# A gated scan that feeds a top-1 mixture of experts: results turned by VectorE in place of TensorE, operands loaded in another order, the routing end reordered

## The chip, the cores and the metric

The kernel runs on one core of a Trainium2 chip. TensorE (PE in the profile) multiplies, VectorE (DVE), ScalarE (ACT) and GpSimd (POOL) do elementwise work, and SyncE (SP) does little but issue transfers. The metric is device time in microseconds of one execution; times before and after are medians of several runs.

## The reference

Two stages follow each other. The first is a decaying linear-attention scan over 4 batches, 8 heads and 768 positions (head width 32, state width 16), in chunks:

```
la  = log(clip(a)); cum = cumsum(la)                 # per chunk
M   = (C @ B.T) * exp(cum_i - cum_j) * causal
y   = M @ x + (C @ state) * exp(cum)
state = exp(sum(la)) * state + sum_j B_j x_j * exp(cum_end - cum_j)
```

Its output, read as 3072 tokens of 256 numbers, goes into eight experts. Each token goes to the expert with the largest logit, in order of arrival, and is dropped beyond the capacity of 768:

```
logits = y @ w_gate;  e = argmax(logits);  gate = softmax(logits)[e]
h   = relu(rows_of_e @ w1[e])          # 256 -> 1024
out[token] = gate * (h @ w2[e])        # 1024 -> 256, put back at the token's row
```

## The kernel before

**Scan.** The work goes over 24 tiles of 128 positions (six per batch), software-pipelined in one loop over `k`: scores and mask of tile k, the product with x of tile k-1, logits and routing of tile k-2. The order of the calls in that loop is the order on every engine (`manual_schedule`). The operands of batch b+1 (`c_n`, `b_n`, `b_s`, the zero-padded `xz`, rows of decays into the tile `both`, rows of `cn` into `cbd`) are issued on SP's queue by `load_part(b + 1, t)` in step t of batch b. Most are `paced`: the transfer waits for the decay product (`ldp`, L392) of the running step. A batch's `b_n` is first read by `scores` (L442), its `xz` by `carry` (L402). The weights of expert 0 are loaded in the same queue in eight pieces, at the steps in `LOADS`; POOL and ACT split the first of them from step 14 on.

**Routing end.** After the last tile, DVE finds each token's expert and slot. A token's slot is turned into two one-hot factors (`hot_a`, `hot_e`, and from the latter `hot_b`), and PE sums their products (`spots`, L836) into the table `who`: for each expert and slot, the token that sits there. The gathers of rows (`fetch`, L169, on POOL's queue) read `who` as indices and `rows_d` in HBM, where each group of tiles has written its rows (L578). The first 128 rows of expert 0 (the "lead") were gathered earlier; `lead_gemm` (L637) and the products at L1111 compute them in single precision in one pass while the rest of the routing runs. Eight matmuls with no use for their result (L1116) follow.

**Experts.** Eight units follow: 296 rows for expert 0, then 424 rows (3 blocks of 128 and one of 40) for each of experts 1 to 7. Operands are split into a high and a low part (`wh`/`wl`, `xh`/`xl`, `hh`/`hl`; ACT makes the high, DVE the low part), and a product is three matmuls: high-high, high-low, low-high. `gemm1` makes eight blocks f of the hidden layer, six matmuls each (L991), through three PSUM banks: ACT writes `hh`, DVE `hl`, and then the bank is free. `gemm2` makes two output halves d, 24 matmuls each (L1015), copied by ACT to `yt` (L1021). Since `yt` has tokens along the free dimension, `finish` turns it back: for each block of 128 tokens two PE transposes (L1061) into PSUM, a DVE multiplication by the gate (L1048) and a scatter of the rows by POOL (L1049). These jobs are the list `after`; `gemm1` of the next unit pops one after each f from 1 on. During `gemm2`, `turned` prepares the next unit's rows (`turned_blocks` is a 32x32 block transpose by DVE of a tile `g4` that came through HBM; then `xh`, `xl`, and with `find` the send targets `oi`), the next weights are split by the list `jobs`, and the rows of the unit after that are gathered. The last unit computes `gemm2` by token (L1073) and has no turn.

## Time and profile before

| | us |
|---|---|
| median of 3 runs (lowest, highest) | 271.59 (270.85, 272.19) |
| the profiled execution, its own time | 269.67 |
| its span in the profile | 267.9 |
| PE busy | 246.7 (92%) |
| DVE busy | 178.6 (67%) |
| ACT busy | 127.6 (48%) |
| POOL busy | 126.5 (47%) |

Times in the profile are microseconds from the span's start. In its rows a line number is a line of the kernel before, followed by the operation, output<-inputs, partitions x elements. A bracket gives the idle time of the engine just before, and what ended it; "issue" stands for a wait for nothing that the profile shows. The scan takes up to about 85 us, the routing end up to about 106 us, the experts the rest.

### The profile page before, as it was taken

What the parts mean: (1) busy time and instruction counts of PE and PEld (TensorE: products, weight loads), DVE (VectorE), ACT (ScalarE), POOL (GpSimd) and SP (SyncE); (2) the same over time, 40 slices, a digit from 0 to 9 for tenths busy, and PEclk for the clock granted to TensorE, in tenths of its full rate; (3) what the DMA queues carried; (4) which work ended last, traced back from release to release, by engine and by line L of the source; (5) the groups of instructions that cost most, each with busy time, mean ns of one, the idle gap of its engine ahead of it and who ended that gap; (6) DMA issues with size and microseconds to landing.
All of it is one profiled execution on the core that took longest, in us unless ns stands there. A gap on an engine that the chain in (4) does not pass through costs nothing.

```text
span 267.9 us, 7098 instructions
## 1 busy us (share of the span) xinstructions
PE 246.7 (92%) x2746; PEld 206.3 (77%) x2747; DVE 178.6 (67%) x453; ACT 127.6 (48%) x289; POOL 126.5 (47%) x165
## 2 busy tenths in 40 slices
PE   7899998799899779999999999999999999999960
PEld 2345655455556777999999999999999999999960
DVE  6699597567795854686695686496496676676210
ACT  2377557358663442573374463383373553644000
POOL 6966225154683154445353485365465385015230
PEclk9999999999999959999999999999999999999995
DMA  6573645956837222494865914853944925101010
GB/s 197 157 193 90 161 112 136 282 157 172 231 129 214 89 97 65 136 348 169 223 260 150 353 52 140 252 231 111 320 158 126 354 75 168 37 2 64 21 46 3
DMA packets 30101, 42.06 MB, mean 157 GB/s; under 512 B 16089, under 2 KB 22075, under 8 KB 28528
## 3 DMA queue, kind: packets, MB, share of 16 engines
q1 hardware_dynamic: 26656, 33.69, 41.1%
q0 software_dynamic: 3280, 7.86, 9.3%
q8 instruction: 23, 0.38, 0.5%
q14 instruction: 14, 0.11, 0.1%
q10 hardware_dynamic: 128, 0.01, 0.0%
HBM read 32.19 MB, written 9.39 MB: 155 GB/s over the span
## 4 chain that ended last, share of the span: by engine, by line
PE 80%; DVE 7%; DMA 3%; issue 3%; ACT 2%; POOL 1%; SPq 0%; POOLq 0%; ACTq 0%; DVEq 0%
PE ps L991 27%; PE ps L1015 23%; PE sp L442 4%; PE ps2f L1073 4%; PE yp L463 4%; PE yp L474 3%; PE pj L481 2%; PE psy L1061 2%; PE dsp L402 2%; PE ps L1111 2%; DMA b_n<-bn 2%; PE ldp L392 1%; DMA c_n<-cn 1%; DVE mz L448 1%; PE yp L412 1%
## 5 line engine op out<-in xcount | busy, mean ns | idle before, releaser
L169 POOL DMA_INDIRECT g<-rows_d,who x28 | 42.7, 1527 | 37.3 <-PE ps L1015 32.6
L994 DVE SCALAR_TENSOR_TENSOR hl<-ps,hh 128x424 fp32r<-128x424 f32 (+1 forms) x64 | 37.3, 583 | 31.5 <-ACT hh L993 31.3
L993 ACT ACTIVATE hh<-ps 128x424 fp32r<-128x424 f32 (+1 forms) x64 | 32.7, 511 | 45.7 <-PE ps L991 45.7
L1049 POOL DMA_INDIRECT out<-yo,oi x31 | 30.6, 987 | 34.1 <-DVE yo L1048 34.1
L1015 PE MATMUL ps<-hh,wh 128*128 128x424 f32 (+1 forms) x112 | 39.0, 348 | 0.0
L1015 PE MATMUL ps<-hh,wl 128*128 128x424 f32 (+1 forms) x112 | 38.8, 346 | 0.0
L1015 PE MATMUL ps<-hl,wh 128*128 128x424 f32 (+1 forms) x112 | 38.7, 346 | 0.0
L991 PE MATMUL ps<-xh,wh 128*128 128x424 f32 (+1 forms) x128 | 36.9, 368 | 0.1
L128 DVE TENSOR_TENSOR wl<-r,wh 128x1024 fp32r<-128x1024 f32 (+1 forms) x32 | 34.9, 1144 | 0.7 <-ACT wh L127 0.7
L991 PE MATMUL ps<-xh,wl 128*128 128x424 f32 (+1 forms) x128 | 34.2, 348 | 0.0
L127 ACT ACTIVATE wh<-r 128x1024 fp32r<-128x1024 f32 (+2 forms) x48 | 34.2, 767 | 0.0
L991 PE MATMUL ps<-xl,wh 128*128 128x424 f32 (+1 forms) x128 | 34.1, 348 | 0.0
L991 PEld LDWEIGHTS ps<-xl,wh 128*128 128x128 f32 x128 | 23.6, 188 | 0.7
L991 PEld LDWEIGHTS ps<-xh,wl 128*128 128x128 f32 x128 | 23.6, 188 | 0.6
L991 PEld LDWEIGHTS ps<-xh,wh 128*128 128x128 f32 x128 | 21.6, 189 | 0.8 <-ACT xh L949 0.4
L1015 PEld LDWEIGHTS ps<-hl,wh 128*128 128x128 f32 x112 | 21.1, 188 | 0.5
L1015 PEld LDWEIGHTS ps<-hh,wh 128*128 128x128 f32 x112 | 21.1, 188 | 0.4
L1015 PEld LDWEIGHTS ps<-hh,wl 128*128 128x128 f32 x112 | 21.0, 188 | 0.4
L448 DVE TENSOR_TENSOR mz<-sp,lx 128x512 f32<-128x512 f32 x24 | 16.5, 686 | 5.3 <-PE sp L442 3.7
L367 POOL TENSOR_TENSOR bpt<-b_s,wt 128x128 f32<-128x128 f32 x22 | 10.0, 455 | 20.9 <-PE dsp L402 20.9
L476 ACT ACTIVATE ys<-yp 128x128 f32<-128x128 f32 x48 | 10.7, 275 | 18.2 <-PE yp L474 18.2
L442 PE MATMUL sp<-cbd,b_n 64*64 64x256 f32 x176 | 15.5, 401 | 2.0 <-issue 1.6
(190 smaller groups left out, 437.9 us busy)
## 6 DMA issues: line engine op xcount, KB each, us to landing
r<-w SPq DMA_DIRECT2D x12, 1024.0 KB, 6.5
r<-w SPq DMA_DIRECT2D x16, 256.0 KB, 5.3
g<-xr_d SPq DMA_DIRECT2D x24, 112.0 KB
rows_d<-rt SPq DMA_DIRECT2D x5, 514.0 KB
xr_d<-g SPq DMA_DIRECT2D x6, 385.5 KB
xz<-x SPq DMA_DIRECT2D x6, 256.0 KB, 6.4
c_n<-cn SPq DMA_DIRECT2D x3, 384.0 KB, 3.2
b_s<-bt SPq DMA_DIRECT2D x3, 384.0 KB, 5.1
```

The source lines that it names most:

```text
L127: act.activation(hi[:, sl], r[:, sl], AF.Copy)
L128: engine.tensor_tensor(out=lo[:, sl], in0=r[:, sl], in1=hi[:, sl].bitcast(F32), op=ALU.subtract)
L169: got = pool.indirect_dma_start(out=g[0:r, s], out_offset=None, in_=rows_d[0:known, :], in_offset=bass.IndirectOffsetOnAxis(ap=index[0:r, ...
L442: pe.matmul(sp[64 * c:64 * c + 64, g, 0:4 * CH], nat(b, "bn", ts.start, ts.stop)[gp], cbd[b % 2][gp, :, ts], start=True, stop=True)
L448: dve.tensor_tensor(out=m.rearrange("p (g h) i -> p g h i", g=2), in0=sp[:, :, 0:4 * CH].rearrange("p g (h i) -> p g h i", h=4), in1=lx.re ...
L463: step[0] = pe.matmul(yps[g][32 * hh:32 * hh + 32, c * CH:(c + 1) * CH], x_z[:, c, h * D:(h + 1) * D], m[:, h], start=c == 0, stop=False, ...
L991: mm = pe.matmul(ps, wv[:, k, fs], xv[:, k], start=i == 0, stop=i == 5)
L993: act.activation(hh[:, f, 0:w], ps, AF.Relu)
L994: dve.scalar_tensor_tensor(out=hl[:, f, 0:w], in0=ps, scalar=0.0, in1=hh[:, f, 0:w].bitcast(F32), op0=ALU.max, op1=ALU.subtract)
L1015: mm = pe.matmul(ps, wv[:, f, ds], hv[:, f, 0:w], start=f == 0 and j == 0, stop=f == NF - 1 and j == 2)
L1049: sc = pool.indirect_dma_start(out=out, out_offset=bass.IndirectOffsetOnAxis(ap=oi[0:r, s:s + 1], axis=0), in_=yo[0:r], in_offset=None, bo ...
L1073: pe.matmul(ps, hv[:, f, sl], wv[:, f, :], start=f == 0 and j == 0, stop=f == NF - 1 and j == 2)
```

## The change

1. `load_part` issues `bt` and `cn` in step 0, `bn` in step 1, and the second part of `xz` in step 4. `LOADS` puts two pieces of expert 0's weights at steps 6 and 7 and the other six at steps 14 to 19.
2. The routing end is written in another order. The last two groups (three tiles and one) share one `hots_of` over four tiles; `hot` can give its two halves to two engines; the last group's rows are written from ACT's queue; all of `lead_gemm` is ahead of the last `spots`; two idle matmuls are added ahead of the last positions.
3. The send targets of all experts are made at once (`oi_all`) ahead of the first unit, together with a cleared `yt_all`; `find` and its four DVE instructions per unit go.
4. `turn` (PE transposes of the rows of units 0 and 1) fills both halves block by block and stores afterwards.
5. `finish` is no longer used for the units. ACT writes `yt_all` padded to 448 columns, DVE turns each half in 32x32 blocks into `yb`, and `assemble` moves the blocks to their partitions with 16 copies of 32 partitions (eight on ACT, eight on DVE, four per job), then four jobs multiply by the gate (DVE and ACT in turn) and scatter. `gemm1` pops from f = 0.
6. The first job of the weight split runs in `turned`, between the block transpose and `xh`.

```diff
-LOADS = (10, 11, 16, 17, 18, 19, 20, 21)
+LOADS = (6, 7, 14, 15, 16, 17, 18, 19)
...
     def turn(g, w, bank, store):
+        both = [bank(w) for k in range(2)]
+        for s in range(-(-w // P)):
+            r = min(P, w - s * P)
+            for k in range(2):
+                pe.transpose(out=both[k][:, s * P:s * P + r], in_=g[0:r, s, k * P:(k + 1) * P], identity=ident[0:r, 0:r])
         for k in range(2):
...
+            store(k, both[k])
...
-            for nm in ((("cn",), ("bt",)) + ((),) * 4)[t]:
+            for nm in ((("bt", "cn"), ("bn",)) + ((),) * 4)[t]:
                 paced(out=loads[b][nm], in_=src_of[nm][:, b])
-            if t in (1, 3):
-                load_xz(b, t // 2, pace=True)
...
-                paced(out=loads[b]["bn"], in_=bn[:, b])
+            if t in (1, 4):
+                load_xz(b, t // 4, pace=True)
...
-        def hot(n0, T, a_, eq, engine):
+        def hot(n0, T, a_, eq, *engines):
...
-                engine.tensor_tensor(out=b_[:, :, v], in0=eq, in1=bc(parts_of[:, n0:n0 + T, v:v + 1], [P, T, E * ks]), op=ALU.mult)
+                engines[v % len(engines)].tensor_tensor(out=b_[:, :, v], in0=eq, in1=bc(parts_of[:, n0:n0 + T, v:v + 1], [P, T, E * ks]), op=ALU.mult)
...
-        weave(mid, [lambda: None, lambda: None] + late)
+        weave(mid, [lambda: None, lambda: None] + late[:-2])
+        warm = p1.tile([P, CBW], F32, name="warm", tag="yp0")
+        for _ in range(2):
+            pe.matmul(warm, ones, cb_s[:, 0:CBW], start=True, stop=True)
...
-        for op in mid[:3]:
+        for op in (mid[0], mid[2], mid[1], mid[3], mid[5], *late[-2:]):
             op()
         last = route_2(*last, at_of(2, E).rearrange("p (t e) -> p t e", t=1))
-        route_3(*last)
+        act.activation(rt[:, 0, 0:DM], pj[:, 0:DM], AF.Copy)
+        route_3(*last, act)
         late = take()
+        for op in (late[1], late[3], late[5]):
+            op()
         while hots:
             list_(*hots.pop(0))
-        lead_gemm()
-        weave(mid[3:], late)
-        hots.append(hot(*known[0], pool))
-        hots.append(hot(*known[1], dve))
+        while lead_f:
+            lead_gemm()
+        both = hots_of(k - 3, 4)
+        for op in (mid[4], late[4], mid[6], late[6], *both[0:3], late[0], late[2], *both[3:]):
+            op()
+        hots.append(hot(*known[0], dve, pool))
...
-        while lead_f:
-            lead_gemm()
...
                     turned_blocks(xt, g4)
+                    if early:
+                        early.pop(0)()
                     act.activation(xh, xt[:, :, 0:w], AF.Copy)
...
-                    if f >= (4 if rush else 1) and after:
+                    if f >= (4 if rush else 0) and after:
                         after.pop(0)()
...
-                    act.activation(yt[:, d], ps, AF.Copy)
-                return yt
+                    act.activation(yt[:, d, 0:w], ps, AF.Copy)
+                    dve.transpose(out=yb[:, d, 0:n], in_=yt[:, d])
+                return yb
...
+            def assemble(yb, w, gate, oi):
+                nf, blocks = -(-w // Q), -(-w // P)
+                y4 = gp.tile([P, blocks, DM], F32, name="y4", bufs=1)
+                src = yb.rearrange("p k (s r c) -> p k s r c", r=4, c=Q)
+                dst = y4.rearrange("p s (k q c) -> p k s q c", k=2, q=4)
+                todo = []
+                for i in range(16):
+                    q, r = divmod(i, 4)
+                    n = -(-(nf - r) // 4)
+
+                    def move(to=dst[r * Q:(r + 1) * Q, :, 0:n, q], of=src[q * Q:(q + 1) * Q, :, 0:n, r], i=i):
+                        if i % 2:
+                            dve.tensor_copy(to, of)
+                        else:
+                            act.activation(to, of, AF.Copy)
+                    todo.append(move)
+                moves = [lambda some=todo[i:i + 4]: [m() for m in some] for i in range(0, 16, 4)]
+                return moves + [lambda s=s, r=min(P, w - s * P): put(y4[:, s], gate, oi, s, r, True) for s in range(blocks)]
...
+                yt_all = gp.tile([P, 2, quarters * Q], F32, name="yt_all", bufs=1)
+                dve.memset(yt_all, 0.0)
+                oi_all = gp.tile([P, E, KW], I32, name="oi_all", bufs=1)
+                dve.tensor_copy(oi_all, who.rearrange("p (e s) -> p e s", e=E)[:, :, 0:KW])
+                if lead:
+                    dve.tensor_copy(oi_all[:, 0, 0:KW - 1], who[:, 1:KW])
+                for i in range(E):
+                    dve.copy_predicated(oi_all[:, i], dead[:, i], nowhere)
...
-                    cur = turned(g_n, *nxt, four.pop(u + 1, None))
                     if nxt[0] != e:
                         jobs = split_weights(nxt[0], *raws[nxt[0]][1:], wpools[nxt[0] % 2])
+                    cur = turned(g_n, *nxt, four.pop(u + 1, None), jobs)
...
-                    after = finish(yt, w, gate, oi)
+                    after = assemble(yb, w, gate, oi)
```

The order of the instructions shows three places. First SP's queue in the scan, where batch 2 is loaded (steps 6 to 11); before:

```order
L338 DMA c_n<-cn 128x768
L338 DMA b_s<-bt 128x768
L338 DMA xz_103<-x 64x512 x2
L220 DMA both<-cums 1x48x64 x6
L353 DMA cbd_101<-cn 16x768 x4
L338 DMA b_n<-bn 128x768
L578 DMA rows_d<-rt 128x4x257
L338 DMA xz_103<-x 64x1024 x2
L338 DMA r<-w 128x512 x2
```

and now:

```order
L339 DMA b_s<-bt 128x768
L339 DMA c_n<-cn 128x768
L339 DMA r<-w 128x512
L339 DMA b_n<-bn 128x768
L339 DMA xz_103<-x 64x512 x2
L339 DMA r<-w 128x512
L221 DMA both<-cums 1x48x64 x6
L352 DMA cbd_101<-cn 16x768 x4
L588 DMA rows_d<-rt 128x4x257
L339 DMA xz_103<-x 64x1024 x2
```

`b_n` has moved ahead of ten small transfers, and the two weight pieces from behind the second `xz` to places ahead of it.

Second, PE at the routing end, the piece around `lead_gemm` (`lead_p`) and the last `spots`; before:

```order
L637 MATMUL lead_p_2177<-lead_h,r 128x128 x4
L836 LDWEIGHTS hot_a
L836 MATMUL spots<-hot_b,hot_a 128x48
...
L857 MATMUL cnt<-lead_run,cb_s 128x8
L637 MATMUL lead_p_2223<-lead_h,r 128x128 x4
L1111 MATMUL ps_2289<-lead_h,r 128x128 x8
```

and now:

```order
L643 MATMUL lead_p_2179<-lead_h,r 128x128 x4
L643 MATMUL lead_p_2185<-lead_h,r 128x128 x4
L844 LDWEIGHTS hot_a
L844 MATMUL spots<-hot_b,hot_a 128x48
...
L870 MATMUL cnt<-lead_run,cb_s 128x8
L1159 MATMUL ps_2294<-lead_h,r 128x128 x8
```

One group of lead matmuls has moved from behind `cnt` to ahead of the last `spots`.

Third, DVE in `gemm1`, where the results of the unit before are put in place; before (unit 2, counted from 0, takes in the results of unit 1):

```order
L994 SCALAR_TENSOR_TENSOR hl<-ps_2756,hh 128x424
L1048 TENSOR_SCALAR yo<-psy,gate 128x256
L994 SCALAR_TENSOR_TENSOR hl<-ps_2774,hh 128x424
L1048 TENSOR_SCALAR yo<-psy,gate 128x256
L994 SCALAR_TENSOR_TENSOR hl<-ps_2791,hh 128x424
```

and now:

```order
L1038 STREAM_TRANSPOSE yb<-yt_all 128x448
L1008 SCALAR_TENSOR_TENSOR hl<-ps_2750,hh 128x424
L1087 COPY y_2739<-yb 32x2x4x32
L1087 COPY y_2739<-yb 32x2x3x32
L1008 SCALAR_TENSOR_TENSOR hl<-ps_2763,hh 128x424
L1087 COPY y_2739<-yb 32x2x4x32
```

Between two `hl` there were 0 or 1 other instructions; now there are two copies in each of the first four gaps and 0 or 1 after that. ACT has the same two copies behind `hh`.

57 lines of the change are left out of this document (32 added, 25 removed).

## The prediction

> **What bounds the kernel now.** I read the page's engine totals, then a table by stretch, then the chain of waits in order of time for the longest stretch, and the instruction rows for the others.
>
> ```profile
> PE 246.7 (92%) x2746; PEld 206.3 (77%) x2747; DVE 178.6 (67%) x453; ACT 127.6 (48%) x289; POOL 126.5 (47%) x165
> 48.00:62.00 14.00, 12.44 (x297) 7.26 (x291) 9.69 (x34) 7.40 (x25) 4.32 (x10) 1.00 0.72 199
> 94.00:95.00 1.00, 0.20 (x1) 0.10 (x1) 0.96 (x4) 0.00 (x0) 0.86 (x2) 0.62 1.01 346
> 96.00:97.00 1.00, 1.00 (x7) 1.00 (x7) 0.00 (x0) 0.00 (x0) 0.00 (x0) 0.50 0.00 0
> 101.00:102.00 1.00, 1.00 (x11) 1.00 (x10) 1.00 (x2) 0.27 (x1) 0.69 (x2) 0.96 0.15 41
> 150.40:169.80 19.40, 19.40 (x106) 18.61 (x105) 13.57 (x24) 9.78 (x16) 11.61 (x8) 1.00 0.48 164
> ```
>
> In a stretch's row stand its length, then PE, PEld, DVE, ACT and POOL busy, and the granted clock. In the experts (last row) PE is busy 19.40 of 19.40 us: a unit costs what PE's instructions cost. In the scan PE lacks 1.56 us of 14. At the routing end it idles around 94 us, and from there to about 101 us it has half its clock.
>
> ```profile
> 121.10 2.33 PE ps L991 x12
> 123.65 1.16 PE ps L991 x6
> 140.17 2.32 PE ps L991 x12
> 142.71 1.16 PE ps L991 x6
> 144.09 1.16 PE ps L991 x6
> 145.47 1.16 PE ps L991 x6
> 146.85 3.45 PE ps L991 x18
> ```
>
> This is the chain in `gemm1`. The first piece at 140.17 ends at 142.49, the next starts at 142.71: 0.22 us for a pair of PE transposes, four times a unit.
>
> **Turn back (part 5).** The page of groups by shape counts the transposes removed, and prices what DVE and ACT do instead:
>
> ```profile
> L1061 PE MATMUL psy<-hd_s,yt 128*128 128x128 f32 x42 | 8.0, 271 | 0.0
> L1061 PE MATMUL psy<-hd_s,yt 128*40 128x128 f32 x14 | 2.7, 272 | 0.0
> L994 DVE SCALAR_TENSOR_TENSOR hl<-ps,hh 128x424 fp32r<-128x424 f32 x56 | 33.6, 599 | 28.9 <-ACT hh L993 28.7
> L245 DVE TENSOR_SCALAR cbd<-hd_s 128x256 f32<-128x256 f32 x4 | 1.1, 343 | 0.0
> L160 DVE STREAM_TRANSPOSE xt<-g 128x896 f32<-128x896 f32 x6 | 6.7, 1109 | 3.7 <-DMA g<-xr_d 3.7
> L993 ACT ACTIVATE hh<-ps 128x424 fp32r<-128x424 f32 x56 | 29.4, 525 | 41.6 <-PE ps L991 41.6
> L499 ACT ACTIVATE rt<-pj 128x256 f32<-128x256 f32 x23 | 8.9, 386 | 8.7 <-PE pj L481 6.6 <-PE pj L497 1.8
> ```
>
> There are 56 transposes; two belong to the lead and stay. The other 54 are 27 pairs. At 0.22 us they are 5.9 us of PE time, all on the chain.
>
> What replaces them runs beside PE. For DVE a unit gets two transposes of 448 (half of 1109 ns each, 1.1 us in all) and eight copies of up to 256 elements. No copy between partition groups is in the trace; the nearest row is L245, 343 ns, so 2.7 us. It loses two of four gate products (about 1.0) and four `find` instructions (about 0.7). DVE comes from 13.6 to some 15.7 us of 18.5. ACT gains eight copies and two products at about 386 ns: 9.8 + 3.9 = 13.7 us. Neither is full over a unit, but four gaps are. There PE makes a block in 1.16 us, while DVE needs 0.60 + 2 x 0.34 = 1.28 and ACT 0.53 + 2 x 0.39 = 1.31, less what neighbours overlap. DVE falls behind by 0.12 a block, 0.5 us in four. Three PSUM banks allow for more:
>
> ```profile
> 159.57 2.33 PE ps L991 x12
> 161.39 0.60 DVE L994 SCALAR_TENSOR_TENSOR hl<-ps,hh 128x424 fp32r<-128x424 f32 x1 [1.62 <-ACT hh L993]
> ```
>
> The first `hl` ends at 161.99, 2.42 us after the unit began; PE needs that bank for the fourth block, 3 x 1.16 = 3.48 us after it. The slack is about 1.05 us. So I cost the copies at nothing. Bounds of a copy: 0.2 us (no lag), and 0.69 us, the row of 512 elements with two inputs, L448 below, at which DVE lags 0.82 a block, 3.3 us in four, and PE loses 3.3 - 1.05 = 2.2 us a unit, 13 us in six.
>
> ```profile
> L448 DVE TENSOR_TENSOR mz<-sp,lx 128x512 f32<-128x512 f32 x24 | 16.5, 686 | 5.3 <-PE sp L442 3.7 <-PE pj L481 1.4
> ```
>
> I take the 256-element row since the size is the same. The weight split ahead of `xh` (part 6) fills the 0.98 us in which DVE waits for `xh`, and no one waits for it: term 0. Sum of this part: -5.9, from -6.2 to +7.
>
> **Loads (part 1).**
>
> ```profile
> 28.80 0.78 PE L442 MATMUL sp<-cbd,b_n 64*64 64x256 f32 x8 [0.39 <-DMA b_n<-bn]
> 47.45 0.78 PE L442 MATMUL sp<-cbd,b_n 64*64 64x256 f32 x8 [1.15 <-issue]
> 54.12 0.38 PE L402 MATMUL dsp<-xz,bpt 128*32 128x128 f32 x2 [1.36 <-issue]
> 70.38 0.65 PE L442 MATMUL sp<-cbd,b_n 64*64 64x256 f32 x4 [0.45 <-issue]
> 35.52 4.72 SPq L220 DMA_DIRECT2D both<-cums  x6
> 40.29 2.14 SPq L353 DMA_DIRECT2D cbd<-cn  x4
> 42.53 1.04 SPq L338 DMA_DIRECT2D b_n<-bn  x1
> ```
>
> PE waits 0.39 us for the first `b_n`. The 1.15 us at 47.45 have no releaser, but stand at the first instruction of batch 2's `scores`, 3.9 us after `b_n` was issued (43.57). I read that as `b_n` too. It is now issued ahead of 4.72 + 2.14 us of small transfers, so both waits go: 1.5 us. The 1.36 and 0.45 us lie in the middle of a group whose first instructions had run, so they aren't operands; I leave them. The second `xz` has a later step, but SP is behind its steps: its queue came to `xz` at 44.21 and `b_n` ahead of it took 1.04. The weight pieces ahead of the small transfers cost SP 0.4 us each and hide there. Term -1.5; bounds +1 (as much as the wait it cures, where a weight piece or `xz` now ends last) and -3.3 (all four waits).
>
> **Routing end (parts 2 to 4).**
>
> ```profile
> 92.35 1.14 PE L637 MATMUL lead_p<-lead_h,r 128*128 128x128 f32 x8
> 94.58 0.20 PE L836 MATMUL spots<-hot_b,hot_a 128*128 128x48 bf16 x1 [1.09 <-POOL hot_b L597]
> 95.52 2.05 PE L637 MATMUL lead_p<-lead_h,r 128*128 128x128 f32 x8
> 98.12 5.23 PE L1111 MATMUL ps<-lead_h,r 128*128 128x128 f32 x32 [0.55 <-ACT got L860]
> 104.65 1.12 PE L156 MATMUL ps<-hd_s,g_first 128*128 128x128 f32 x6
> 105.25 0.97 ACT L949 ACTIVATE xh<-ps 128x296 fp32r<-128x296 f32 x2 [1.58 <-PE ps L156]
> 105.76 0.96 DVE L950 TENSOR_TENSOR xl<-ps,xh 128x296 fp32r<-128x296 f32 x2 [3.71 <-issue]
> 93.28 0.37 SPq L578 DMA_DIRECT2D rows_d<-rt_last  x1
> 99.95 1.15 POOL L169 DMA_INDIRECT g_first<-rows_d,who  x1 [0.30 <-DVE lead_oi L876]
> DMA to landing us min/median/max: 2.9/3.1/3.3
> ```
>
> The group of 2.05 us moves into PE's idle 1.09 us, so L1111 can start about 1.5 us earlier, at 96.6. From 98.12 to the end of the turn (105.77) are 7.65 us: 104.2. The last gather of `g_first` starts at 99.95 and lands by 103.2 (the last row), and perhaps 0.5 us earlier, since the last rows' reciprocal is five short instructions further ahead. So PE still ends last. If the clock stayed up, the lead's 2.05 would be 1.14 again and L1111 shorter by about as much in proportion (half of three halved microseconds, 1.5); then the gather would end it, near 103.2. The new `turn` has both halves ready at its end, so the second `xh` no longer runs beside it: +0.4. Range of the gain: 0 (`who` late) to 2.2; I take 1.7. The cleared `yt_all` and the targets are some 2.5 us of DVE, in the 3.71 us in which it idles ahead of `xl`; without that cover they would cost up to 2.5.
>
> [...]
>
> **Sum.** -5.9 - 1.5 - 1.7 = -9.1. The profiled execution took 269.67 us, of which 267.9 are the span: 260.6. It was 1.9 us below the median of the runs, 271.59; on the median's scale 262.5.
>
> **Rivals.**
> 1. *DVE's filled gaps set the pace.* For it: 1.28 against 1.16 us, and the copies' price is a guess. Against: 1.05 us of slack, and five lighter gaps after the four. With copies of 0.55 us the lag is 4 x 0.54 = 2.2, the loss 1.1 us a unit, 6.6 in six: 271.6 - 9.1 + 6.6 = 269.1.
> 2. *Only the transposes go.* Loads and gathers end as before, as the unexplained waits and the gather at 99.95 allow: 271.6 - 5.9 = 265.7.
> 3. *Slower: GpSimd and the copies exclude each other.*
>
> ```profile
> 213.99 4.61 DVE L128 TENSOR_TENSOR wl<-r,wh 128x1024 fp32r<-128x1024 f32 x4
> 214.57 4.91 POOL L169 DMA_INDIRECT g<-rows_d,who  x1 [1.26 <-PE ps L1015]
> 219.79 0.95 POOL L169 DMA_INDIRECT g<-rows_d,who  x1 [0.30 <-issue]
> ```
>
> A gather that takes 0.95 us otherwise took 4.91 beside four DVE instructions, and the last gather runs into the next `gemm1`, which begins at 217.7. If a copy there had to wait for such a gather, DVE would lag by up to 4 us; beyond the slack 3 us a unit, 18 in six: 271.6 - 9.1 + 18 = 280. It is slower from a loss of 1.5 us a unit on, a wait of 2.6. Against it: in these rows POOL waited, and DVE's four took their usual time. [...]
>
> **Chances.** Forecast 0.62 (its own range 259.5 to 265), rival 1 0.13, rival 2 0.13, rival 3 0.06, something that leaves the time alone 0.06. The range reaches from 259.0 (loads -3.3, end -2.2, transposes -5.9 less the median's scatter) to 268.0, over rival 2 and half of rival 1. About 0.5% (1.4 us) is what a measurement can tell from no change. Faster: 0.62 + 0.13 + most of rival 1, 0.87; same 0.07; slower 0.06.
>
> **What would show it.** In the profile after: a unit of 18.5 us with no gap between blocks of `gemm1`; copies near 0.34 us, and `hl` less than 1 us later at the fifth block; no wait ahead of `scores` of tiles 6 and 12; L1159 beginning near 96 us less what the scan won; last gather before the turn. The forecast is wrong if PE waits for `hl` in `gemm1` (copies too dear), if waits of the scan come back at other instructions, or if the end of the routing is set by the gather at its old distance.

## The result

The changed kernel takes 261.0 us (median of four runs: 259.1, 260.1, 261.9 and 263.8), the kernel before 271.9 us beside it (270.9 to 274.6). The ratio is 0.956, with a 95% interval from 0.945 to 0.967. The prediction was 262.5 us, within 259.0 to 268.0. Ratios and their intervals, here and below, leave out every execution that took over 1.5% longer than the fastest of its kernel, so they are not the quotients of the medians. The profiled execution is the longest of the four, 263.77 us with a span of 261.9; it has half the TensorE clock for 10 us at the routing end. Against the profiled execution before (span 267.9) it gains 6.0 us.

Line numbers move with the edit: `gemm1` L991 is now L1005, `gemm2` L1015 is L1031, the lead's end L1111 is L1159, `lead_p` L637 is L643, `hl` L994 is L1008, the gather L169 is L170. New are the DVE transpose L1038, the copies L1087 (DVE) and L1089 (ACT), and the products L1068 (DVE) and L1066 (ACT). First the engine totals of the profile after, then two stretches (length, then PE, PEld, DVE, ACT and POOL busy, granted clock): the scan's stretch that stood in the prediction, and one unit of the experts.

```profile
PE 242.7 (93%) x2694; PEld 203.3 (78%) x2695; DVE 189.3 (72%) x484; ACT 153.6 (59%) x358; POOL 125.5 (48%) x164
```

```profile
48.00:62.00 14.00, 13.03 (x349) 7.93 (x348) 10.55 (x40) 8.71 (x29) 5.68 (x14) 1.00 0.66 185
138.00:156.60 18.60, 18.60 (x98) 18.01 (x97) 15.16 (x28) 13.67 (x25) 9.39 (x7) 1.00 0.63 196
```

A unit costs 18.6 us where it cost 19.4, and PE is still busy in all of it. DVE is at 15.2 of 18.6 us and ACT at 13.7 (forecast 15.7 and 13.7). The groups by shape show what the copies cost:

```profile
L1087 DVE COPY y<-yb 32x256 f32<-32x256 f32 x24 | 6.8, 285 | 0.7
L1087 DVE COPY y<-yb 32x192 f32<-32x192 f32 x28 | 7.1, 254 | 0.5
L1089 ACT ACTIVATE y<-yb 32x256 f32<-32x256 f32 x24 | 9.9, 414 | 0.9 <-DVE yb L1038 0.5
L1089 ACT ACTIVATE y<-yb 32x192 f32<-32x192 f32 x28 | 10.1, 360 | 0.3
```

**Where the 6.0 us of the two profiles lie.** The scan ends (first `lead_p` group) at 86.13 instead of 87.64: -1.5. From there to the first `gemm1` it takes 18.45 us instead of 18.08: +0.4. From there to PE's last matmul 147.8 instead of 153.1: -5.3. What follows takes 9.5 instead of 9.1: +0.4, whose cause stays open.

**The scan.** These are the waits of PE without a releaser that are left in the profile after; behind them stands what the transfer queue named "instruction" moved in the window from 82.3 to 83.4 us (packets, MB, share):

```profile
31.61 0.45 PE L474 MATMUL yp<-ct,state 32*64 32x64 f32 x10 [0.76 <-issue]
52.18 0.38 PE L402 MATMUL dsp<-xz,bpt 128*32 128x128 f32 x2 [0.54 <-issue]
84.72 0.31 PE L463 MATMUL yp<-mz,xz 128*32 128x64 f32 x6 [1.42 <-issue]
```

```profile
q8 instruction: 1, 0.02, 5.5%
```

No `scores` waits any more. All three waits stand inside a group whose first matmuls had run. The second is 0.8 us shorter than its like before, the third 0.9 us longer; in sum such waits take 2.7 us here and 2.3 before. The transfer of a piece of 16 KB in that queue (22 of them, 0.36 MB, in the whole profile) ends 1.4 to 1.5 us before each of them does. The author read these pieces as PE's program; the experiments return to this.

**The routing end.** First the clock by stretch in the profile after, then rows of PE and the last gather of `g_first` in order of time:

```profile
81.89:85.31 3.42, 2.00 (x56) 1.72 (x55) 1.32 (x7) 0.84 (x4) 0.00 (x0) 1.00 0.47 173
85.31:95.55 10.24, 9.49 (x66) 8.80 (x57) 6.14 (x39) 2.69 (x13) 0.97 (x2) 0.50 0.30 101
95.55:104.58 9.03, 7.47 (x67) 6.37 (x65) 6.29 (x30) 4.00 (x11) 6.36 (x6) 1.00 0.20 53
```

```profile
86.13 2.08 PE L643 MATMUL lead_p<-lead_h,r 128*128 128x128 f32 x8 [0.46 <-ACT lead_h L632]
97.28 3.84 PE L1159 MATMUL ps<-lead_h,r 128*128 128x128 f32 x32 [0.31 <-ACT got L871]
100.59 1.49 POOL L170 DMA_INDIRECT g_first<-rows_d,who  x1 [0.30 <-issue]
103.83 0.31 PE L156 MATMUL ps<-hd_s,g_first 40*128 40x40 f32 x2 [0.81 <-DMA g_first<-rows_d,who]
```

The wait of 1.42 us leaves PE busy for 2.00 of 3.42 us, and from the end of that stretch on it has half the clock for 10.24 us, at the very place where the closing order was to become denser. Each `lead_p` group takes 2.1 us instead of 1.1, and the last gather, not PE, ends the routing end.

**One unit lost.** In the last unit of this execution the tokens came late. Rows of DVE, of ACT and of PE's weight loads:

```profile
225.50 1.11 DVE L161 STREAM_TRANSPOSE xt<-g 128x896 f32<-128x896 f32 x1 [2.52 <-SPq L1221]
233.22 0.55 DVE L1008 SCALAR_TENSOR_TENSOR hl<-ps,hh 128x424 fp32r<-128x424 f32 x1
234.69 0.60 DVE L1008 SCALAR_TENSOR_TENSOR hl<-ps,hh 128x424 fp32r<-128x424 f32 x1 [0.34 <-ACT hh L1007]
236.06 0.60 DVE L1008 SCALAR_TENSOR_TENSOR hl<-ps,hh 128x424 fp32r<-128x424 f32 x1 [0.18 <-ACT hh L1007]
234.14 0.53 ACT L1007 ACTIVATE hh<-ps 128x424 fp32r<-128x424 f32 x1
234.69 0.79 ACT L1089 ACTIVATE y<-yb 32x256 f32<-32x256 f32 x2
235.50 0.53 ACT L1007 ACTIVATE hh<-ps 128x424 fp32r<-128x424 f32 x1
238.07 0.30 PEld L1005 LDWEIGHTS ps<-xh,wh 128*128 128x128 f32 x2 [0.29 <-DVE hl L1008]
```

`xt` starts 5.4 us before the unit's first matmul (230.90), where in four of the five others it is 7.3 to 8.0. The first `hl` is then late, and since ACT needs 0.53 + 0.79 us and a little idle time for a filled block, `hl` follows at 1.36 to 1.37 us a block beside PE's 1.16. PE waits, and the unit takes 21.2 us, where later kernels show 20.7 for it on time (both up to the start of PE's last group of matmuls). `hl` has the same pace in units on time; there it starts early enough that PE does not wait.

### The profile page after: what moved, and what is told of

Same layout as the page of the kernel before. It is cut to its first block, busy times and chain, and to the rows that moved or that the text cites. A ratio compares the mean times of both kernels' runs of the same rounds, so it can differ in the third digit from the quotient of the medians.

```text
span 261.9 us, 7081 instructions
## 1 busy us (share of the span) xinstructions
PE 242.7 (93%) x2694; PEld 203.3 (78%) x2695; DVE 189.3 (72%) x484; ACT 153.6 (59%) x358; POOL 125.5 (48%) x164
## 5 line engine op out<-in xcount | busy, mean ns | idle before, releaser
L1069 POOL DMA_INDIRECT out<-yo,oi_all x31 | 32.2, 1037 | 56.8 <-DVE yo L1068 50.4
L1008 DVE SCALAR_TENSOR_TENSOR hl<-ps,hh 128x424 fp32r<-128x424 f32 (+1 forms) x64 | 37.2, 582 | 14.7 <-ACT hh L1007 13.8
L170 POOL DMA_INDIRECT g<-rows_d,who x28 | 40.2, 1437 | 13.2 <-PE ps L1031 6.9
L1031 PE MATMUL ps<-hl,wh 128*128 128x424 f32 (+1 forms) x112 | 39.0, 348 | 0.0
L1031 PE MATMUL ps<-hh,wh 128*128 128x424 f32 (+1 forms) x112 | 39.0, 348 | 0.0
L1031 PE MATMUL ps<-hh,wl 128*128 128x424 f32 (+1 forms) x112 | 38.9, 347 | 0.0
L1005 PE MATMUL ps<-xh,wh 128*128 128x424 f32 (+1 forms) x128 | 34.9, 353 | 0.4 <-ACT xh L960 0.4
L127 ACT ACTIVATE wh<-r 128x1024 fp32r<-128x1024 f32 (+2 forms) x48 | 34.8, 767 | 0.1
L1005 PE MATMUL ps<-xl,wh 128*128 128x424 f32 (+1 forms) x128 | 34.5, 350 | 0.0
L1005 PE MATMUL ps<-xh,wl 128*128 128x424 f32 (+1 forms) x128 | 34.3, 349 | 0.0
L1005 PEld LDWEIGHTS ps<-xh,wh 128*128 128x128 f32 x128 | 23.4, 188 | 2.2 <-DVE hl L1008 0.8
L1005 PEld LDWEIGHTS ps<-xl,wh 128*128 128x128 f32 x128 | 23.7, 188 | 0.7
L1005 PEld LDWEIGHTS ps<-xh,wl 128*128 128x128 f32 x128 | 23.7, 188 | 0.5
L1089 ACT ACTIVATE y<-yb 32x192 f32<-32x192 f32 (+2 forms) x56 | 21.3, 380 | 1.3 <-DVE yb L1038 0.5
L1031 PEld LDWEIGHTS ps<-hh,wl 128*128 128x128 f32 x112 | 21.1, 188 | 0.6
L1031 PEld LDWEIGHTS ps<-hh,wh 128*128 128x128 f32 x112 | 21.0, 188 | 0.6
L1031 PEld LDWEIGHTS ps<-hl,wh 128*128 128x128 f32 x112 | 21.1, 188 | 0.4
```

The source lines that it names most:

```text
L127: act.activation(hi[:, sl], r[:, sl], AF.Copy)
L170: got = pool.indirect_dma_start(out=g[0:r, s], out_offset=None, in_=rows_d[0:known, :], in_offset=bass.IndirectOffsetOnAxis(ap=index[0:r, ...
L1005: mm = pe.matmul(ps, wv[:, k, fs], xv[:, k], start=i == 0, stop=i == 5)
L1008: dve.scalar_tensor_tensor(out=hl[:, f, 0:w], in0=ps, scalar=0.0, in1=hh[:, f, 0:w].bitcast(F32), op0=ALU.max, op1=ALU.subtract)
L1031: mm = pe.matmul(ps, wv[:, f, ds], hv[:, f, 0:w], start=f == 0 and j == 0, stop=f == NF - 1 and j == 2)
L1069: sc = pool.indirect_dma_start(out=out, out_offset=bass.IndirectOffsetOnAxis(ap=oi[0:r, s:s + 1], axis=0), in_=yo[0:r], in_offset=None, bo ...
```

## The experiments

Twelve further runs were made, in three sets, each set on one chip; one of them is the changed kernel once more. "Lead to gemm1" is the time from the first `lead_p` group to the first `gemm1`. "Late" is the loss of units against 18.6 us (20.7 for the last), from the starts of `gemm1` in the profiled execution.

| kernel | median us, before beside it | ratio (95%) | first lead_p | lead to gemm1 | late, us |
| --- | --- | --- | --- | --- | --- |
| before (first profile) | 271.6 | | 87.64 | 18.08 | units of 19.4 |
| changed | 261.0, 271.9 | 0.956 (0.945 to 0.967) | 86.13 | 18.45 | 0.5 |
| TensorE turns back | 269.8, 273.6 | 0.984 (0.980 to 0.989) | 86.75 | 18.78 | units of 19.45 |
| old loads | 265.6, 273.6 | 0.963 (0.958 to 0.968) | 86.43 | 19.54 | 1.1 |
| old end | 266.5, 273.6 | 0.974 (0.971 to 0.978) | 86.65 | 18.70 | 2.4 |
| turn back alone | 269.3, 273.6 | 0.983 (0.977 to 0.988) | 92.35 | 18.83 | 0.6 |
| changed again | 265.4, 273.3 | none | 89.10 | 18.47 | 2.4 |
| three a gap | 261.3, 273.3 | 0.965 (0.954 to 0.976) | 87.14 | 15.82 | 0.1 |
| copies on DVE | 271.7, 273.3 | 0.997 (0.990 to 1.004) | 85.67 | 15.85 | units of 20.16 |
| code shift | 262.4, 273.3 | 0.968 (0.954 to 0.983) | 88.03 | 15.85 | 1.1 |
| late split | 266.1, 272.7 | 0.977 (0.968 to 0.986) | 85.16 | 15.84 | 3.6 |
| before, code shift | 270.9, 272.7 | 1.003 (0.996 to 1.011) | 89.01 | 18.70 | units of 19.4 |
| three a gap, shift | 263.9, 272.7 | 0.978 (0.973 to 0.983) | 89.31 | 15.94 | 1.3 |
| loads alone | 271.9, 272.7 | 1.004 (0.993 to 1.014) | 87.52 | 22.12 | units of 19.4 |

### The first set: one part undone, one part alone

TensorE turns back (loads, end and early split as changed):

```
-                    if f >= (4 if rush else 0) and after:
+                    if f >= (4 if rush else 1) and after:
...
-                    dve.transpose(out=yb[:, d, 0:n], in_=yt[:, d])
-                return yb
+                return yt
...
-                    after = assemble(yb, w, gate, oi)
+                    after = finish(yb, w, gate, oi)
```

> The changed kernel with its results turned back by TensorE again (transposes in four gaps of gemm1, no DVE transposes and no copies); loads, routing end, weight split and oi_all as changed. Theory (the turn back is worth the gaps it fills): a unit takes 19.35 us again instead of 18.6, six units 4.5 us, and the time is 0.973 to 0.980 of the kernel before (265.5 us beside 271.9; by the prediction's 5.9 us for 27 pairs 266.9). Rival (the units shrank for another reason, the weight split ahead of xh or the targets made at once): units stay near 18.6 us and the ratio near 0.956. For the last unit, which gained nothing in the changed kernel: if the copies cost it what the transposes had cost, PE no longer waits for hl at its blocks 5 to 7 and it takes 21.7 us all the same; if its xt is late for another reason, the waits stay and it takes about 0.7 us longer.

Ratio 0.984. Units take 19.45 us again and the last one 21.56. On-time units of the changed code take 18.58 to 18.63 and 20.7 us (its first two 14.69 and 18.58, here 14.69 and 19.22); summed over the eight, the transposes cost 5.7 us, 0.21 us a pair. The theory holds for the units, and the rival falls: it is the turn back that shrank the units. The ratio is a little above the expected 0.973 to 0.980.

Old loads (the changed kernel with LOADS and load_part of before):

```
-LOADS = (6, 7, 14, 15, 16, 17, 18, 19)
+LOADS = (10, 11, 16, 17, 18, 19, 20, 21)
...
-            for nm in ((("bt", "cn"), ("bn",)) + ((),) * 4)[t]:
+            for nm in ((("cn",), ("bt",)) + ((),) * 4)[t]:
...
```

> The changed kernel with the loads of before (LOADS and load_part); all else as changed. Theory of the prediction: the two waits ahead of scores of tiles 6 and 12 come back, 0.4 and 1.15 us, and the time is 1.5 us above the changed kernel, 0.961 of the kernel before. Rival (the new stalls in the middle of groups, 0.76 us near 31.6 and 1.42 us near 84.7 in the changed kernel, are the price of the new order of loads): those two go when the loads go back, and the ratio is 0.956 or lower.

Ratio 0.963; its interval overlaps that of the changed kernel, so it does not price the loads. The profiled execution also had half the clock for 3.4 us in its first unit, which took 16.2 us instead of 14.7. One of the two waits came back, twice as long; the other did not. The stalls inside groups stayed (1.09, 1.15 and 0.67 us), so they aren't the price of the new loads. The first row is of this kernel, the next two are of the kernel with the turn back alone, which has the old loads too:

```profile
29.24 0.78 PE L443 MATMUL sp<-cbd,b_n 64*64 64x256 f32 x8 [0.82 <-DMA b_n<-bn]
```

```profile
31.57 0.78 PE L442 MATMUL sp<-cbd,b_n 64*64 64x256 f32 x8 [3.01 <-DMA b_n<-bn]
51.25 0.78 PE L442 MATMUL sp<-cbd,b_n 64*64 64x256 f32 x8 [0.88 <-issue]
```

The wait for `b_n` varies from 0.4 to 3.0 us between executions with the old loads. The two without a releaser at the first `scores` of batch 2 (1.15 us before, 0.88 here) aren't waits for program: the last piece had come 4.2 and 3.8 us before they ended. The wait for `b_n` is in none of the ten profiles with the new loads (in one of these, the changed kernel again, `scores` waits 0.91 us for `cbd`).

Old end (the changed kernel with the closing order, the queue of the last rows and the turn of before):

```
-        weave(mid, [lambda: None, lambda: None] + late[:-2])
-        warm = p1.tile([P, CBW], F32, name="warm", tag="yp0")
-        for _ in range(2):
-            pe.matmul(warm, ones, cb_s[:, 0:CBW], start=True, stop=True)
+        weave(mid, [lambda: None, lambda: None] + late)
...
-        hots.append(hot(*known[0], dve, pool))
+        hots.append(hot(*known[0], pool))
+        hots.append(hot(*known[1], dve))
...
```

> The changed kernel with the routing end of before (order of the closing instructions, queue of the last rows, no two idle matmuls, turn of the first tokens half by half). Theory of the prediction: gemm1 of the first unit begins 1.7 us later and the time is 1.7 us above the changed kernel, 0.962 of the kernel before. Rival 1 (what the new end wins in order it loses to the half clock): no difference, 0.956. Rival 2 (the clock at the end is set by the stall near 84 us, not by the closing order): the clock in the stretch from 82 to 102 us differs from execution to execution in both kernels, and with it the end, by more than 1.7 us.

Ratio 0.974, five us above the changed kernel's by the ratios, more than any theory gave. The profile shows two differences. From the first lead group to `gemm1` it takes 18.70 us, 0.25 more than the changed execution. And its third unit takes 20.96 us: `xt` starts only 3.5 us ahead, and PE waits for `wl`, then for `hl`.

```profile
140.09 0.46 PE L993 MATMUL ps<-xh,wl 128*128 128x424 f32 x1 [0.24 <-DVE wl L128]
143.93 0.66 PE L993 MATMUL ps<-xh,wh 128*128 128x424 f32 x2 [0.67 <-DVE hl L996]
```

So this run doesn't price the closing order by itself, and beside the 0.971 that the changed kernel has in the second set it is hardly slower. Why the tokens of that unit came later with the old end stays open.

Turn back alone (the kernel before with the DVE transposes, the copies and their buffers):

```
-                    yt = gemm2(e, w, hh, hl, jobs)
-                    after = finish(yt, w, gate, oi)
+                    yb = gemm2(e, w, hh, hl, jobs)
+                    after = assemble(yb, w, gate, oi)
...
```

> The kernel before with the turn back alone (DVE transposes, sixteen copies in the first four blocks, product and scatter in the last four); loads, routing end, find per unit and the weight split behind xl as before. Theory: six units of 18.6 us instead of 19.35, 4.4 us (5.9 by the prediction), ratio 0.978 to 0.984. Rival (the copies need the lighter DVE of the other edits: targets made at once save four short instructions a unit, and the earlier split evens its load): PE waits for hl in gemm1, units of 19 us or more, ratio 0.99 or above.

Ratio 0.983. Units take 18.41 to 18.60 us, but for one of 19.05 (its `xt` began 7.1 us ahead), so the copies do not need the other edits. The scan of this execution ended 4.7 us later than that of before (3.0 us went to the `b_n` above, and twice in it the clock was halved for 3.4 us), so that the span was equal to that of before, while from the first `gemm1` on PE ended 5.6 us sooner; without the late unit that is 6.1.

### The second set: slack, pace, code

The changed kernel once more, with no edit:

> The changed kernel once more, beside the three below on one chip, for a second profile. Theory (the time that the scatter of its runs spans comes from the half clock near 85 us and from late tokens of single units): the ratio is again 0.956 within 0.01, units without a wait for hl take 18.5 to 18.6 us, and a unit that takes longer has a DVE transpose of xt that waited over 2 us for a DMA. Rival (the slow last unit belongs to the kernel): unit 7 again has PE waiting for hl in its fifth to eighth block and no late xt.

On this chip it took 265.4 us (260.9 to 268.6), beside 273.3. That is 0.971 by the medians, with no interval, and not the expected 0.956 within 0.01. The eight runs of the changed kernel on two chips have a median of 262.9 us. The theory holds for the units: those on time take 18.6 us, and the three slow ones (19.01, 19.41, and the last with 21.86) have an `xt` that began 5.5, 5.0 and 4.7 us ahead. The scan shows something new, in rows of PE and POOL:

```profile
74.78 0.53 PE L402 MATMUL dsp<-xz,bpt 128*32 128x128 f32 x8 [2.13 <-POOL bpt L367]
73.15 1.13 POOL L170 DMA_INDIRECT lead_h<-rows_d,lead_slot  x1 [3.94 <-DVE sel L595]
74.30 0.42 POOL L367 TENSOR_TENSOR bpt<-b_s,wt 128x128 f32<-128x128 f32 x1
```

The lead's gather starts 2 us after its list is there (`lead_slot`, 70.83), and `bpt` stands behind it on POOL. It reads `rows_d`, whose last part SP issued at 65.56, right ahead of three weight pieces. The landing of these rows took 6.7 us, as the line of their issue says:

```profile
rows_d<-rt SPq DMA_DIRECT2D x1, 514.0 KB, 6.7
```

They landed at 72.3, behind the list, and the gather began 0.9 us later. The same wait is 1.67 us in the code shift and 1.47 with three a gap and the shift, where the rows landed 0.4 and 0.2 us behind the list (7.3 and 7.6 us after their issue) and the gather began 0.9 us after the landing as well; it is 0.28 in the other profiles with the new loads (in that of the changed kernel the rows took 6.6 us and were there 0.9 us ahead of the list). In all three the clock was halved for 3.4 us soon behind that wait. That the weight pieces made the rows late is not shown.

Three copies a block (3, 3, 3, 3, 4 instead of 4, 4, 4, 4):

```
-                moves = [lambda some=todo[i:i + 4]: [m() for m in some] for i in range(0, 16, 4)]
+                cut = (0, 3, 6, 9, 12, 16)
+                moves = [lambda some=todo[i:j]: [m() for m in some] for i, j in zip(cut, cut[1:])]
```

> The sixteen copies in five blocks of gemm1 (three, three, three, three and four) where the changed kernel has four blocks of four; the four products follow one block later. By the rows of the kernels run so far a block with four copies takes ACT 0.53 + 0.79 = 1.32 us and DVE 0.60 + 0.55 = 1.15, beside 1.16 for PE; with three ACT has 1.1 to 1.2. Theory (ACT's filled blocks cannot catch up, so that a unit whose tokens came late stays at 1.36 us a block for all four): late units lose at most 0.3 us instead of 0.5 to 0.8, the others nothing, and the time is that of the changed kernel less 0 to 1 us. Rival (the copies cost nothing in any unit): no difference at all, and the later products and scatters push the gathers of the next tokens back: 0 to 1 us longer.

261.3 us. Tokens that began 5.4 and 5.2 us ahead cost 0 and 0.1 us, where with four copies a block 5.4 and 5.0 us ahead cost 0.5 and 0.8. So a part of what a late unit pays is the filled blocks; not all of it, as tokens 4.05 us ahead cost 1.3 us with three copies a block as well (below). In time it can't be told from the changed kernel.

All copies on DVE:

```
-                        if i % 2:
-                            dve.tensor_copy(to, of)
-                        else:
-                            act.activation(to, of, AF.Copy)
+                        dve.tensor_copy(to, of)
```

> All sixteen copies of a unit on DVE, none on ACT, else the changed kernel. DVE then needs 0.60 + 4 x 0.285 = 1.74 us a block beside 1.16 for PE: a lag of 0.58 a block, 2.3 us in four. Theory of the prediction (three banks give a slack of 1.05 us): PE waits for hl in the fourth to sixth block and a unit takes 1.2 to 1.3 us longer, 19.85 us; six units 7.5 us, ratio 0.98 to 0.985. Rival 1 of the prediction with no slack at all: 2.3 us a unit, 14 us, slower than before. The other end (only DVE's sum over a unit counts, 18.1 of 18.6 us): nothing, 0.956.

```profile
139.41 0.60 DVE L1008 SCALAR_TENSOR_TENSOR hl<-ps,hh 128x424 fp32r<-128x424 f32 x1
140.04 1.11 DVE L1086 COPY y<-yb 32x256 f32<-32x256 f32 x4
141.18 0.60 DVE L1008 SCALAR_TENSOR_TENSOR hl<-ps,hh 128x424 fp32r<-128x424 f32 x1
143.60 0.65 PE L1005 MATMUL ps<-xh,wh 128*128 128x424 f32 x2 [0.34 <-DVE hl L1008]
145.39 0.65 PE L1005 MATMUL ps<-xh,wh 128*128 128x424 f32 x2 [0.36 <-DVE hl L1008]
```

`hl` comes every 1.77 us, PE needs 1.165. At the fifth block `hl` is 2.3 us late (the first step is 1.65 us). Units take 20.16 us, 1.56 more than 18.6 and more than the expected 1.2 to 1.3. The slack is 2.3 - 1.56, about 0.75 us. The slack of three banks is real but smaller than the 1.05 of the prediction, and the ratio of 0.997, above the expected 0.98 to 0.985, is what rival 1 of the prediction looks like when copies are dear: the whole gain is gone.

Part of the difference is a reading in the prediction. It counted the first `hl`'s end (161.99) from 159.57, where a piece of the chain begins, but the unit began at 159.41:

```profile
159.41 0.55 PE L991 MATMUL ps<-xh,wh 128*128 128x424 f32 x2
```

From there the first `hl` ends after 2.58 us, and the same sum gives 3.48 - 2.58 = 0.90.

Code shift (178 more instructions of PE at the start, the rest unchanged):

```
-        keep_warm(WARM, "lj")
+        keep_warm(WARM - 7, "lj")
+        small = p1.tile([P, 512], F32, name="small", tag="lj")
+        for i in range(96):
+            pe.matmul(small[0:32, 0:64], warm_s[:, 0:32], warm_s[:, 0:64], start=True, stop=True)
```

> Seven of the nineteen idle matmuls at the start are replaced by 96 of 64 columns, which take about the same time; nothing else is changed, and PE's program is 178 instructions longer ahead of the scan. Theory (the stalls in the middle of a group, with no releaser, are PE waiting for its program, which comes in pieces of 16 KB, 256 instructions): every such stall moves by the same number of instructions, 39 matmuls later than in the changed kernel; the stall after 26 of the 32 matmuls of the last yp (1.42 us, 84.72) is gone from there, PE stays busy around 84 us and the clock is not halved at 85; where it stays up, who comes 1 to 2 us earlier and so does the first gemm1: 0.950. Rival (the stalls are operands, or DMA traffic at that time): the stall at the 27th matmul of the last yp stays, 0.5 to 1.4 us, and so does the ratio, 0.956.

The stall at the 27th matmul of the last `yp` is gone, and so are those at the old places of the earlier tiles. New ones stand elsewhere (1.05 us at 24.13, 0.44 at 50.01, 0.57 at 70.74). From 80.3 us on the clock stays up (it was halved for 3.4 us ahead of that, behind the wait for `bpt`), and from the first lead group to `gemm1` it takes 15.85 us; three kernels without the shift whose last `yp` had a stall of at most 0.58 us show the same. The theory holds as far as the stalls are a matter of position in the program: counted in PE's matmuls and weight loads, those of the changed execution stand behind 931, 1936 and 3451 of them and these behind 687, 1940 and 2947, in both cases steps of some 250 or multiples of it, with other work at the same counts. The ratio, 0.968, is not the expected 0.950: the small matmuls put the first tiles back by 0.7 us, and `bpt` cost 1.4 more than usual.

### The third set: what is left

Late split (part 6 undone):

```
-                    if nxt[0] != e:
-                        jobs = split_weights(nxt[0], *raws[nxt[0]][1:], wpools[nxt[0] % 2])
-                    cur = turned(g_n, *nxt, four.pop(u + 1, None), jobs)
+                    cur = turned(g_n, *nxt, four.pop(u + 1, None))
+                    if nxt[0] != e:
+                        jobs = split_weights(nxt[0], *raws[nxt[0]][1:], wpools[nxt[0] % 2])
```

> The changed kernel with the weight split behind xl again, as before (part 6 undone). Prediction's term for that part: 0, so units of 18.6 us where xt starts 7 us or more ahead of the unit, and the ratio of the changed kernel (0.956 to 0.965). Rival (the early split is what keeps DVE and ACT even, and without it the last pieces of the split run into the filled blocks): wl or hl is waited for at the start of gemm1, units of 19 us and more, 3 us or more in all, 0.97 and above. Second rival (one piece of the split ahead of xh makes late tokens later still): units with late tokens lose less than 0.4 us here, where they lost 0.4 to 0.9 in the changed kernel.

```profile
130.05 1.11 DVE L161 STREAM_TRANSPOSE xt<-g 128x896 f32<-128x896 f32 x1 [3.69 <-DMA g<-xr_d]
135.63 0.46 PE L1005 MATMUL ps<-xh,wl 128*128 128x424 f32 x1 [0.60 <-DVE wl L128]
139.46 0.66 PE L1005 MATMUL ps<-xh,wh 128*128 128x424 f32 x2 [0.68 <-DVE hl L1008]
```

Units on time take 18.58 to 18.62 us, so for them the term is 0, as forecast. Late ones pay more: 6.1 us ahead costs 0.9 us (5.9 ahead cost nothing with the early split), 4.2 ahead costs 2.7; in the turn back alone, which has the late split too, 7.1 ahead cost 0.6. The ratio is 0.977, above the forecast's 0.956 to 0.965, and the loss of 3.6 us with PE waiting for `wl` and `hl` is what the first rival said. So the early split does not shorten a unit on time; by these three units it lowers the price of late tokens, for which the prediction had no term.

The kernel before, with the code shift:

```
-        keep_warm(WARM, "lj")
+        keep_warm(WARM - 7, "lj")
...
+        for i in range(96):
+            pe.matmul(small[0:32, 0:64], warm_s[:, 0:32], warm_s[:, 0:64], start=True, stop=True)
```

> The kernel before with the same 178 instructions more at its start, nothing else changed. From the end of the last yp to the first gemm1 the kernel before and the two other kernels with the old closing order took 18.1 to 18.7 us from the first lead group on, with 6.8 to 10.2 us of half clock; the new order took 15.85 in three kernels in which the clock stayed up and 18.5 to 19.5 in four in which it did not. Theory A (the closing order of before halves the clock by its own idle time near 94 us): the stall at the 27th matmul of the last yp moves away, yet the clock is halved near 94 us and the stretch stays at 18 to 18.7 us; ratio 0.995 to 1.005. Theory B (the stall for code alone sets the clock there): the clock stays up, the stretch falls to 16.5 us or less and the ratio to 0.99 or below, so that the new order would be worth next to nothing by itself.

```profile
73.75 0.43 PE L466 MATMUL yp<-mz,xz 128*32 128x64 f32 x5 [2.45 <-issue]
```

```profile
q8 instruction: 1, 0.02, 5.8%
```

```profile
94.24:97.64 3.40, 2.04 (x22) 1.74 (x21) 2.65 (x15) 0.38 (x1) 0.86 (x2) 1.00 0.45 155
97.64:104.46 6.82, 6.27 (x30) 5.98 (x29) 3.78 (x15) 2.81 (x7) 4.79 (x5) 0.50 0.17 46
```

First a row of PE in this kernel, then the instruction queue in the window from 71.2 to 72.4 us, then two stretches ahead of and behind the change of clock. No stall stands near 86 us, and yet the clock is halved, after a stretch with PE busy for 2.04 of 3.40 us: theory A, in this one execution. Behind the old closing order the clock was halved in all five kernels that have it: in four it fell 4.7 to 8.6 us behind the first lead group, in the last run below it had fallen ahead of that group, behind a stall of 1.39 us. Only this kernel and the kernel before had no such long stall close ahead.

Three a block with the code shift:

```
-                moves = [lambda some=todo[i:i + 4]: [m() for m in some] for i in range(0, 16, 4)]
+                cut = (0, 3, 6, 9, 12, 16)
+                moves = [lambda some=todo[i:j]: [m() for m in some] for i, j in zip(cut, cut[1:])]
...
-        keep_warm(WARM, "lj")
+        keep_warm(WARM - 7, "lj")
...
+        for i in range(96):
+            pe.matmul(small[0:32, 0:64], warm_s[:, 0:32], warm_s[:, 0:64], start=True, stop=True)
```

> The changed kernel with the copies in five blocks (three, three, three, three, four) and with the 178 instructions more at its start. Theory (late units lose no more than 0.1 us, no stall for code near 84 us, clock up from there on): 0.95 to 0.955 of the kernel before, 1 to 2 us less than the changed kernel, and runs that lie closer together. Rival (the stalls for code only move to other places and cost the same in sum, and the clock is halved elsewhere): the time of the five-block kernel without the shift, 0.96 to 0.965.

Ratio 0.978, and six runs within 263.3 to 265.3. The clock stayed up at the routing end (15.94), and one unit whose tokens began 4.05 us ahead lost 1.3 us. But the scan ended at 89.31: a stall of 1.93 us at 72.21, 1.47 for `bpt` with 3.4 us of half clock soon behind it, and the small matmuls. Of the theory, the clock, the missing stall near 84 us and the closer runs came true, the price of a late unit and the time did not. The rival's mechanism holds, since the stalls only moved, but the time lies above its range too (0.96 to 0.965). No version here beats the changed kernel by more than the measurement tells.

The kernel before, with the new loads alone:

```
-LOADS = (10, 11, 16, 17, 18, 19, 20, 21)
+LOADS = (6, 7, 14, 15, 16, 17, 18, 19)
...
-            for nm in ((("cn",), ("bt",)) + ((),) * 4)[t]:
+            for nm in ((("bt", "cn"), ("bn",)) + ((),) * 4)[t]:
...
```

> The kernel before with the loads of the change alone (LOADS and load_part). Prediction's term: 1.5 us, ratio 0.9945, by the two waits ahead of scores of tiles 6 and 12 (0.39 and 1.15 us before; 0.82 and 0.88 to 3.0 in the two other kernels with the old loads), which should be gone. Rival (rows of the list wait behind the weight pieces, as in two of the kernels with the new loads, where bpt came 1.4 to 1.8 us later near 75 us): the gain is given back there, ratio 1.0.

Ratio 1.004, with the forecast's 0.9945 just inside the interval: no gain that can be told from none. In the profile no `scores` waits for `b_n`, as expected. But the stalls inside groups come to 4.15 us here (0.50, 1.42, 0.84, 1.39), where before had 2.29, and the clock is halved for 20.5 us from 85.9 on, so that the stretch to `gemm1` takes 22.12 us. The waits that the loads cure are gone in every profile; what they are worth in one execution is less than what stalls and clock move it by.

## Why the prediction was right, and where it was not

**Turn back: -5.9 forecast, -5.7 measured on units on time.** The chain, the 27 pairs and the price of a copy held: 0.25 to 0.29 us on DVE for 0.34, 0.36 to 0.41 on ACT for 0.386. Without the other edits it was 6.1. "I cost the copies at nothing" holds for tokens on time. It holds narrowly: the slack is 0.75 to 0.9 us, and four filled blocks use 0.65 of it (in the unit of 137.86 the first `hl` ends at 140.45 and the fifth at 145.75, 5.30 us later, where four blocks of PE take 4.66). The pace of a filled block is ACT's, 1.36 us, as the 1.31 of the forecast said.

**What the forecast left out: tokens on time.** It took the arrival of `xt` as given. Units of 18.6 us leave less time for the same chain of transfers, and the four scatters, now in the last four blocks, hold POOL when the next gathers are due (rows under "Rivals": the scatter of 150.23, then the gather of 151.81). Before, POOL was free and waited for PE:

```profile
151.73 1.06 POOL L169 DMA_INDIRECT g<-rows_d,who  x1 [2.27 <-PE ps L1015]
```

In the changed kernel the first gather for the fifth unit starts at 151.81 and the unit at 175.07, 23.3 us later; before it was 151.73 and 178.88, 27.2 us. With four copies a block a unit pays nothing at 5.9 us ahead, 0.4 at 5.5, 0.8 at 5.0, 1.05 at 4.8 and 2.4 at 3.5. That took 0.5 us back in the profiled execution and 2.4 in the second one.

**Loads: -1.5 forecast, -1.5 in the two profiles.** Both waits were `b_n`, as read: they are gone in all ten profiles with the new loads. To leave the 1.36 and 0.45 us alone was right; they are stalls for code (a piece's transfer ends 1.5 and 1.3 us before they do). The upper bound, "where a weight piece or `xz` now ends last", would have happened in three of the ten, if the late rows of the lead were put down to the weight pieces, which is not shown; these rows cost 1.2 to 1.9 us. Alone, the edit showed no gain beyond its scatter, so the 1.5 is shown as waits that are gone and not as time.

**Routing end: -1.7 forecast, +0.4 in the profiled execution, -2.2 where the clock stayed up.** The step that failed is "L1111 can start about 1.5 us earlier": with the scan's gain it would have been at 95.1, and it started at 97.28. The forecast moved a group into idle time at the clock before, and did not see that a stall of the scan could halve the clock under the new order. Its 1.7 is a value between the 1.1 of its steps at the old clock (1.5 less 0.4) and the 2.2 with the clock up (2.6 less 0.4). With the clock up, in five of nine profiles with the new order, the stretch takes 15.8 to 15.9 us, 2.2 less than the 18.08 of before, and the gather ends it, as the prediction said for that case. In the other four it takes 18.5 to 19.5. Those four had a stall of 0.67 to 1.50 us in the last `yp`, the five had 0.58 us or none.

Half the clock lasted 3.4, 6.8, 10.2 or 20.5 us each time in these profiles, but for the one at the very end. PE was not idle all through the stretch ahead of it: it was busy for 2.00 of 3.42 us in the changed kernel, and for 2.04 of 3.40 in the kernel before with the code shift.

**Rivals.** Rival 1 was right on the place and wrong on the extent: filled gaps set the pace only in late units, and with all copies on DVE, where a block's four take as long as the two of 0.55 us in this rival, a unit lost 1.56 us where the rival said 1.1, and the whole gain was gone. Rival 2 is off by 4.7 us on the medians (265.7 against 261.0); but in the profiled execution its routing end came true, and of the loads no run shows a gain in time. Rival 3 is not seen: a gather takes 3.15 us beside two weight splits on DVE, which keep their usual time (2.34 us for the two, 1.20 for one in the mean of the profile), and two copies beside the gather of 214.43 take 0.55 us as elsewhere (0.285 for one in the mean). In the other profiles a few copies beside the end of a gather took up to 0.49 us instead of 0.28, far from the 4 us of that rival.

```profile
150.23 1.28 POOL L1069 DMA_INDIRECT out<-yo,oi_all  x1 [0.30 <-issue]
151.81 3.15 POOL L170 DMA_INDIRECT g<-rows_d,who  x1 [0.30 <-PE ps L1031]
151.69 2.34 DVE L128 TENSOR_TENSOR wl<-r,wh 128x1024 fp32r<-128x1024 f32 x2
214.43 0.95 POOL L170 DMA_INDIRECT g<-rows_d,who  x1 [0.31 <-issue]
214.90 0.55 DVE L1087 COPY y<-yb 32x256 f32<-32x256 f32 x2
```

**What the forecast said it would show.** A unit of 18.5 us without gaps: 18.6, seen. Copies near 0.34: 0.25 to 0.29 on DVE, 0.36 to 0.41 on ACT. `hl` less than 1 us later at the fifth block: 0.65, seen. No wait ahead of `scores`: seen. L1159 near 96 less the scan's gain: no, 97.28. Last gather before the turn: no in every kernel with the new order, PE waits 0.6 to 0.8 us for it. The total was near all the same, and that is in part luck. The forecast was -9.1; the change is worth 10.9 us by the medians on the first chip, 6.0 by the two profiles, and 7.9 by the medians of the second set. The turn back is shown; the routing end gives 2.2 or nothing as the clock falls, late tokens take 0.1 to 2.4, and the 1.5 of the loads is in no time.

## What to carry to other kernels

The work that was moved into PE's shadow cost nothing here as long as its input was on time (units of 18.6 us with PE busy in all of it); so price the slack that such work uses up, here 0.65 of 0.75 to 0.9 us, and ask which transfer eats the rest when the loop gets shorter. Where a wait has no releaser and stands inside a group of equal instructions, look for the transfer of a piece of program ahead of it before looking for an operand: here all 41 of 0.4 us or more had one that ended 1.2 to 1.6 us earlier. And before the order of a stage is judged by one profile, look at the granted clock in it: the same order took 15.85 or 18.45 us here.
